# A second searched order for a fused convolution and mixer kernel, with three fewer pairs of blocks on ScalarE sums of squares

## The chip, the cores and the metric

The kernel runs on one core of one Trainium2 chip. The metric is the device time of one execution in microseconds (us); the kernel before takes 234.74 us (median of three, 234.25 to 235.0). The profiled execution took 234.25 us, and its trace spans 232.4 us from the first to the last instruction, so about 1.9 us of the time lie outside the span.

## What is computed

Two blocks follow each other on a sequence of S = 2048 rows of D = 512 numbers. The first is a long convolution with gates (A), the second a token mixer with an MLP (B), each behind a layer norm and with a residual sum. Cut to what matters:

```python
def A(q, k, v, shift_k, ssm_k, ssm_D):        # q is layernorm(x)
    k_shift = sum over 4 taps of the shifted k times shift_k
    kv = k_shift * v
    y = irfft(rfft(kv padded to 2S) * rfft(ssm_k padded to 2S))[:S]
    return q * (y + kv * ssm_D)

def B(x, w1, w2, w3, w4):
    h = gelu(layernorm(x) @ w1)
    g0..g3 = the four quarters of h's columns, moved by +1, -1, +2, -2 rows
    x1 = x + concat(g0..g3) @ w2
    return x1 + gelu(layernorm(x1) @ w3) @ w4          # w3: 512 x 1792, w4: 1792 x 512

h = x + A(layernorm(x), ...)
out = h + B(layernorm(h), ...)
```

## The kernel before

The Fourier transforms are done as matrix products in two steps each. The kernel builds a list of some 760 small tasks (a group of matmuls, one eviction, one load, one store), each with a closure that emits its instructions and with the engines that may run it. A long string, `ORDER`, then names every task by its number and the engine that gets it: P is TensorE, V VectorE, A ScalarE, G GpSimd, D the DMA queue of SyncE. A search on a host has made this string. Every engine executes its own tasks strictly in the order of the string, so a task whose input isn't there holds up all later tasks of the same engine, the DMA queue included.

```python
    def emit(self):
        made = set()
        for x in ORDER.split():
            n, e = int(x[:-1]), {o[0]: o for o in self.t[int(x[:-1])]["opts"]}[x[-1]]
            assert self.t[n]["deps"] <= made
            self.t[n]["fn"](e)
            made.add(n)
```

The names used below for the tasks of the convolution, for block groups `bl` or frequencies `kh`:

- h, k, v, q: loads. kf: a quarter of k that is loaded transposed by the DMA. F, K, FE, KE: first transform step of the filter and of kv and its eviction from PSUM; S, X: shifted k on TensorE and its product with v on VectorE; N, NE: transposes of k; FX, KX: exchanges over DMA between the two steps.
- G, GE, W, A, P, V, VE, VX: second step, product of the spectra (P, two VectorE operations), inverse step on TensorE (V), its eviction (VE) and the exchange back (VX). qs: row statistics of q.

Every PSUM tile of this part comes from one ring of four (`big`), so a task of TensorE also waits until the tile four allocations earlier is evicted. For an eviction the order chooses the engine:

```python
    def copy(e, o, i):
        if e == "A":
            nc.scalar.copy(o, i)
        else:
            nc.vector.tensor_copy(o, i)
```

In the mixer and MLP part, blocks of 128 rows pass through: J/I (last inverse step), Y (scale, ScalarE), H (residual, VectorE), statistics, hb (normalised h), LT/TE (its transpose), W (w1, TensorE), U (gelu), X (w2), S (x1), lb (normalised x1), L/E (its transpose), M (w3), G (gelu), O (w4), R, Z (sums on VectorE) and ZS (store of the output block). The variance of h and of x1 is taken in one of two ways, chosen per pair of blocks p by `HA` and `XA`:

```python
    HP, LP = 2, 1
    HA, XA = 4, (1, 2)
    # ... cut ...
    def summed(name, b, src, early, **kw):
        i = slice(b % 2, b % 2 + 1)
        if early:
            kw["accum_out"] = pair(name + "s", b // 2, 2, bufs=8)[:, i]
        nc.vector.scalar_tensor_tensor(out=src, **kw)
        if not early:
            stats(name, b, src)          # bn_stats and bn_aggr, both on VectorE

    def squares(name, b, src):           # task Q or SQ, only for early pairs
        def f(e):
            # ... cut ...
            nc.scalar.activation(jk[:], src, ACT.Square, bias=pair(name + "s", b // 2, 2, bufs=8)[:, i], scale=-float(D),
                                 accum_out=pair(name + "q", b // 2, 2, bufs=8)[:, i])
        return f
```

The transposes of the first `HP` = 2 pairs of h (blocks 0 to 3) and of the first pair of x1 are done on TensorE; all later ones go out to a scratch in HBM and come back through the transposing DMA:

```python
                if p < HP:
                    task(("LT", c), {"PE": 0.24}, transposes(("hb", c)), [("hb", c)], take="pt")
                    task(("TE", c), {"A": 0.48, "V": 0.33}, tcopy(("hb", c), hnT, c), drop=("LT", c))
                else:
                    task(("LT", c), {"D": 0.5}, stored(("hb", c), NB + c), [("hb", c)], lat=LAND)
            if p >= HP:
                task(("TE", b), {"D": 1.35}, flipped(hnT, NB + b - 1, 2, (b - 1) * P), [("LT", b - 1), ("LT", b)], lat=LAND)
```

The sum of an output block and its store are two tasks:

```python
            task(("Z", g, i), {"V": 0.7}, summed_up(g, i), [("R", bs[i])], drop=("O", g, i))
            task(("ZS", g, i), {"D": 0.4}, store(g, i), [("Z", g, i)], lat=2.0)
```

The product with w3 and its gelu have 56 tasks each (8 pairs of blocks by 7), the product with w4 has 17. PSUM gives the mixer part a ring of six tiles for matmuls and one of two for transposes.

Of the kernel before, what the change touches and what calls it, by code (L numbers as in the profile page):

```python
# [31 lines left out]
KB = 1024  # L32

ORDER = """
2D 4D 1D 39P 3D 41P 40A 12G 45P 42V 59P 5D 46A 14G 43P 60V 57P 44A 11G 7D 36P 58V 30P 13G 37A 52P 31V 48P 15G 53A 50P 6D
49A 61P 51V 54P 62A 69D 32P 55V 63P 33A 74P 64V 0D 76P 75V 8D 65P 77V 67P 66A 70P 16V 20G 68A 9D 82P 71V 17A 10D 34P 83V
27P 35A 98P 18V 21P 28A 72P 275V 19G 47D 99A 277V 22A 280V 102P 84P 302A 73V 103A 276V 92P 85V 86P 93A 78P 38D 281V 87A
283V 122P 23P 79V 123A 25P 56D 24A 26V 124P 100P 125A 282V 88P 80P 101A 284V 29D 285G 274V 89A 278V 90P 279G 81V 126P
91A 128P 129V 127A 112P 95D 114P 113A 96D 104P 115V 132D 140P 105A 110P 97D 141V 134P 111A 130D 116P 135V 106D 148P 117A
150P 94D 149V 136P 151A 107D 154P 137V 118D 142P 155A 138P 133D 143V 139V 152P 109D 164P 121D 153A 146P 165V 162P 108D  # L40
147A 190P 131D 163V 174P 191A 119D 158P 120D 175A 178P 159V 184P 179A 156P 192V 160P 185A 168P 180V 157A 193P 161A 169V
208P 194A 181P 186V 209A 196P 195D 182V 170P 197A 187P 210V 171A 183D 202P 176P 188A 198V 172P 203A 189D 211P 177V 173A
199P 204V 212A 214P 226P 215A 200V 213D 205P 227A 216V 201D 220P 206A 228V 221A 217P 207D 232P 222V 218A 229P 233A 244P
219D 230V 144P 245A 223P 234V 145A 231D 238P 166P 224A 246V 235P 239A 225D 250P 167V 236A 247P 240V 251A 262P 237D 248A
241P 252V 263A 256P 249D 242V 253P 257A 264V 268P 243D 254A 269A 258V 255D 265P 270V 266A 259P 293V 267D 260A 271P 288V
298P 261D 272A 289V 286V 273D 299P 303D 292V 300P 301P 287V 358P 304D 294V 307G 290V 359P 295V 306D 291G 360A 296V 365A
361V 297G 383A 308P 366V 388A 364A 384V 309P 369A 367P 389V 368P 334A 305D 362P 370V 387A 391P 335V 371G 339A 310A 337P
373G 340V 315A 372V 392A 376V 342P 316V 406P 343A 393V 377D 338A 374V 394G 311V 407P 375D 319A 317P 344V 396G 318P 408A
395V 397V 312P 431A 345G 409V 341P 398D 314A 378D 347G 412A 399A 320V 346V 446P 351V 321G 432V 348A 400D 429A 352P 323G
447P 353A 410P 322V 413V 467A 327G 349P 379P 450A 401D 324G 350A 328P 416V 381P 380A 430V 417G 448A 325P 329A 354P 419G  # L50
326A 433V 418V 420V 465A 356P 451V 434G 421D 422A 330P 355A 436G 423D 357A 435V 332P 439V 437G 382A 466V 440D 402P 331A
333A 438D 404P 403A 449V 424D 485P 405A 482P 452V 486V 453G 441D 497P 483V 487A 500P 455G 498V 484A 425P 501V 499A 427P
488V 426A 468V 489G 444P 502A 428A 442P 490V 445A 503V 491V 511P 504G 494A 469V 454V 458V 470G 456V 443A 492P 459D 505V
495P 512V 513P 493A 457D 472G 496A 523P 508A 514V 593P 509D 525P 460D 594A 524V 587P 595P 588A 526V 583P 596A 591P 527V
584A 597V 528G 463P 506V 592A 471V 475V 461P 473A 529V 598V 476D 532G 464A 585P 515V 474D 530V 462A 516G 531D 589P 586A
533D 517V 535P 518G 520A 537P 590A 477D 536V 599P 507D 538V 534D 519D 539V 521D 480P 540G 600V 602P 541V 544V 481A 601D
542V 545D 510D 543D 659P 522D 603V 655P 660A 604D 661P 656A 546D 611P 662A 664V 609P 663V 612A 637P 610A 627P 638A 683P
628A 671P 684A 685V 675P 672A 615P 686V 676A 679P 616A 631P 680A 649P 632A 607P 650A 617P 608A 639P 618A 620V 657P 619V
640A 642V 653P 658A 641V 478P 654A 629P 479A 605P 630A 547P 606A 571P 548V 559P 549P 572V 633P 613P 560V 634A 573P 614A
550V 673P 624P 674A 551V 574V 552G 575V 553V 554V 576G 635P 625V 556G 651P 577V 580V 636A 626D 578A 581D 561P 557D 652A  # L60
643P 579D 562V 563V 555D 564G 582D 665P 565V 568V 566G 644V 569D 645D 567D 668P 666V 667D 570D 749P 669V 745P 750A 751V
670D 737P 752V 746A 739P 738A 747P 740A 741P 748A 743P 742A 677P 744A 621P 678A 558D 756P 622V 623D 699P 757V 705P 758D
700A 703P 706A 707V 697P 708V 704A 695P 698A 701P 696A 646P 702A 717P 647V 721P 718A 648D 727P 722A 725P 728A 730V 719P
729V 726A 715P 720A 723P 716A 693P 724A 681P 694A 734P 682A 709P 735V 736D 731P 710V 711D 712P 732V 733D 690P 713V 714D
687P 691V 692D 753P 688V 689D 759P 754V 755D 760V 761D
"""

class Plan:
# [23 lines left out]
def kernel(  # L92
# [462 lines left out]
    xh1, x1 = hbm, q_sb  # L555

    HP, LP = 2, 1
    HA, XA = 4, (1, 2)
    pools = {}
    scr = ctx.enter_context(tc.tile_pool(name="scr", bufs=1, space=DRAM)).tile([2 * NB, P, D], BF16, name="scr")  # L560

# [348 lines left out]
```

## Time and profile before

| | us |
|---|---|
| time, median of three | 234.74 |
| span of the trace | 232.4 |
| TensorE busy | 217.2 |
| VectorE busy | 149.1 |
| ScalarE busy | 136.4 |
| GpSimd busy | 43.5 |

The page divides the span into 40 slices. TensorE's row alone looks full throughout, but a matmul that fills a stage paced by somebody else counts as busy as well, so the rows of the other engines have to be read beside it. The granted TensorE clock is full in every slice. All bulk transfers are issued by SyncE on one queue; they moved 34.9 MB. Three stages can be told apart: up to about 83 us the convolution, from there to about 102 us the start of the mixer, and after that the mixer and the MLP, which end at 229.4 us on TensorE.

### The profile page before, as it was taken

The page shows a single profiled execution, that of the slowest core. Times are in us where ns is not written, and L with a number is a line of the kernel's source. Part 1 is how long each engine was busy: PE and PEld are TensorE (multiplying, and loading weights), DVE is VectorE, ACT ScalarE, POOL GpSimd, SP SyncE. Part 2 cuts the span into 40 slices and gives each one's busy share as a digit, 9 for nine tenths or more (in the row PEclk, how much of TensorE's full clock was granted, in tenths as well). Part 3 has the DMA queues.
Part 4 walks back from the last instruction along what each step waited for, and adds up shares of the span by engine and source line. Part 5 has one row for each costly group of instructions (what it writes and reads, how often), then busy time and mean ns, then how long its engine had stood idle before and what let it go on. Part 6 is the DMA issues. An engine that isn't in the chain of part 4 may idle for free. (4 is left out here: it accounts for less than half of the span.)

```text
span 232.4 us, 4643 instructions
## 1 busy us (share of the span) xinstructions
PE 217.2 (93%) x1820; PEld 129.4 (56%) x1835; DVE 149.1 (64%) x331; ACT 136.4 (59%) x199; POOL 43.5 (19%) x80
## 2 busy tenths in 40 slices
PE   7999799999999988969999998999999999999994
PEld 2465344443332334557668567886645867874442
DVE  6775898999999987899898656007953130302221
ACT  3848869999999739968867235762220615440000
POOL 4931303000000132782435200000320000000000
PEclk9999999999999999999999999999999999999999
DMA  6999995971343599654333767000054300001111
GB/s 168 383 260 312 419 420 234 399 305 65 131 171 140 181 309 369 251 109 132 57 92 70 203 154 75 0 3 0 1 164 132 68 23 14 23 3 45 45 35 44
DMA packets 31079, 34.90 MB, mean 150 GB/s; under 512 B 17745, under 2 KB 26066, under 8 KB 29522
## 3 DMA queue, kind: packets, MB, share of 16 engines
q1 hardware_dynamic: 30912, 34.61, 47.7%
q8 instruction: 14, 0.23, 0.4%
q14 instruction: 7, 0.06, 0.1%
q10 hardware_dynamic: 146, 0.01, 0.0%
HBM read 12.59 MB, written 5.51 MB: 78 GB/s over the span
## 5 line engine op out<-in xcount | busy, mean ns | idle before, releaser
L778 ACT ACTIVATE ra<-mm 128x512 bf16<-128x512 f32 x56 | 33.4, 597 | 45.0 <-PE mm L772 45.0
L772 PE MATMUL mm<-rc,rb 128*128 128x256 bf16 x448 | 50.9, 273 | 1.0 <-DMA rc<-scr 1.0
L787 PE MATMUL mm<-rt,ra 128*128 128x512 bf16 (+1 forms) x232 | 49.2, 366 | 0.3
L772 PEld LDWEIGHTS <-rb 128*128 128x128 bf16 x448 | 43.8, 98 | 8.0 <-DMA rc<-scr 1.3
L794 DVE TENSOR_TENSOR ob<-mm,rd 128x512 bf16<-128x512 f32 (+1 forms) x17 | 11.2, 660 | 46.0 <-PE mm L787 46.0
L787 PEld LDWEIGHTS <-ra 128*128 128x128 bf16 x238 | 23.3, 98 | 24.5
L612 DVE SCALAR_TENSOR_TENSOR q_sb<-rd,cr,mm 128x512 bf16<-128x512 bf16 x16 | 11.7, 734 | 18.9 <-PE mm L733 18.7
L507 PE MATMUL pv<-rb,rt 64*128 64x512 bf16 x128 | 17.2, 378 | 1.1 <-ACT rb L269 0.5
L708 PE MATMUL mm<-rc,rf 128*128 128x256 bf16 x128 | 15.1, 273 | 1.9 <-DMA rc<-scr 1.9
L269 ACT CAST rb<-pw 128x1024 bf16<-128x1024 f32 x16 | 16.7, 1093 | 0.0
L269 ACT CAST ra<-pc 128x1024 bf16<-128x1024 f32 x14 | 13.6, 1021 | 2.8 <-PE pc L331 2.7
L733 PE MATMUL mm<-rf,rb 128*128 128x512 bf16 x60 | 14.9, 379 | 0.3
L386 PE MATMUL pk<-diag,rb 128*128 128x256 bf16 (+3 forms) x108 | 14.9, 285 | 0.3
L708 PEld LDWEIGHTS <-rf 128*128 128x128 bf16 x128 | 12.4, 98 | 3.9 <-issue 2.0
L714 ACT ACTIVATE rb<-mm 128x512 bf16<-128x512 f32 x16 | 9.2, 605 | 8.0 <-PE mm L708 6.9
L269 ACT CAST rb<-pv 128x1024 bf16<-128x1024 f32 x12 | 13.1, 1094 | 0.3 <-PE pv L507 0.2
L612 DVE SCALAR_TENSOR_TENSOR rd<-q_sb,qmv,z 128x512 bf16<-128x512 bf16 x16 | 12.1, 772 | 1.7 <-ACT z L599 1.7
L599 ACT ACTIVATE z<-mm,qrs 128x512 f32<-128x512 f32 x16 | 10.4, 706 | 4.6 <-PE mm L588 4.6
L386 PEld LDWEIGHTS <-rb 128*128 128x128 bf16 x112 | 9.4, 98 | 6.2 <-issue 1.7
L395 DVE TENSOR_TENSOR xk<-pk,rb 128x1024 bf16<-128x1024 f32 x8 | 9.7, 1212 | 4.9 <-DMA rb<-in_A_v_dram 2.6
L269 ACT CAST rc<-ph 128x1024 bf16<-128x1024 f32 x11 | 10.9, 1019 | 2.7 <-PE ph L331 2.6
L507 PEld LDWEIGHTS <-rt 64*128 64x128 bf16 x128 | 5.9, 94 | 11.4 <-issue 5.0
(170 smaller groups left out, 303.7 us busy)
## 6 DMA issues: line engine op xcount, KB each, us to landing
rd<-rc SPq DMA_DIRECT2D x16, 256.0 KB, 4.9
rc<-ra SPq DMA_DIRECT2D x16, 256.0 KB, 2.5
ra<-rb SPq DMA_DIRECT2D x16, 256.0 KB, 2.4
ra<-in_A_ssm_k_dram SPq DMA_DIRECT2D x4, 512.0 KB, 5.9
rb<-in_A_v_dram SPq DMA_DIRECT2D x2, 1024.0 KB, 8.6
q_sb<-in_A_q_dram SPq DMA_DIRECT2D x2, 1024.0 KB, 10.7
out_dram<-ob SPq DMA_DIRECT2D x15, 128.0 KB, 1.8
rt<-in_B_w_dram SPq DMA_DIRECT2D x1, 1792.0 KB, 9.5
```

The costliest lines, as they stand in the source:

```text
L269: nc.scalar.copy(o, i)
L386: nc.tensor.matmul(pk[:, i, P * (m + lo):P * (m + hi + 1)], lhsT=kT[:, c, b, KX0:] if b >= 0 else kT[:, c, NB + b, KX0 - 1:KX0 - 1 + P], r ...
L395: nc.vector.tensor_tensor(out=tl["xk", bl][:, :, cs].rearrange("p b (c x) -> p b c x", c=2), in0=tl["pk", bl, ch][:].rearrange("p c (b x) ...
L507: nc.tensor.matmul(ps[:, t, :], lhsT=tt[hs, min(x, 2), kh, :], rhs=pr[hs, x // 2, x % 2, :], start=(x == 0), stop=(x == 3))
L599: nc.scalar.activation(z[:], tl["y", b][:], ACT.Identity, bias=1.0, scale=qrs[:, b:b + 1])
L612: nc.vector.scalar_tensor_tensor(out=src, **kw)
L708: nc.tensor.matmul(pw_[:, j * 256:(j + 1) * 256], lhsT=w1_sb[:, k, m * P:(m + 1) * P], rhs=hnT[:, k, p * 256:(p + 1) * 256], start=(k == 0 ...
L733: nc.tensor.matmul(px[:], lhsT=shifted(m, b), rhs=w2_sb[:, m, :], start=(m == 0), stop=(m == DC - 1))
L772: nc.tensor.matmul(pg[:, j * 256:(j + 1) * 256], lhsT=w3_sb[:, k, fc * P:(fc + 1) * P], rhs=lnT[:, k, g * 256:(g + 1) * 256], start=(k == ...
L778: nc.scalar.activation(gbuf[:, g % 4, 2 * f:2 * f + 2, :], tl["g", g, f][:].rearrange("p (j x) -> p j x", j=2), ACT.Gelu_apprx_tanh)
L787: nc.tensor.matmul(po[:, 0:n], lhsT=gbuf[:, g % 4, fc, i * P:(i + 1) * P], rhs=w4_sb[:, fc, lo:lo + n], start=(fc == 0), stop=(fc == FC - 1))
L794: nc.vector.tensor_tensor(out=ob[:, 0:n], in0=tl["o", 2 * g + i, lo][:, 0:n], in1=xh1[:, order[2 * g + i], lo:lo + n], op=ADD)
```

## The change

The string is replaced by the result of another search, in which the output stores are steps of their own that are issued when their sum is ready. The kernel before has the same tasks for the sums and stores (Z and ZS above); what differs in the diff is the string and the two constants that choose how the variances are taken. `HA` goes from 4 to 3 pairs of h and `XA` from the pairs 1 and 2 of x1 to the pair 1 alone. Nothing else changes. The same values are computed, with four sums of squares fewer on ScalarE and four statistics more on VectorE.

The diff, with all but the first line of each string cut:

```diff
 ORDER = """
-2D 4D 1D 39P 3D 41P 40A 12G 45P 42V 59P 5D 46A 14G 43P 60V 57P 44A 11G 7D 36P 58V 30P 13G 37A 52P 31V 48P 15G 53A 50P 6D
-... (33 more lines)
+3D 2D 1D 48P 4D 54P 49A 14G 52P 55V 41P 5D 53A 13G 45P 42V 43P 46A 12G 7D 34P 44A 11G 36P 35V 59P 37A 15G 30P 60V 57P 6D
+... (33 more lines)
 """
@@ -555,7 +555,7 @@
     HP, LP = 2, 1
-    HA, XA = 4, (1, 2)
+    HA, XA = 3, (1,)
     pools = {}
```

Decoded, the parts of the two strings that the prediction speaks of (task names as above, the engine in front):

```
SyncE, loads       before: h2 k0 h1 h3 k1 v0 k2 kf3 h0 v1 q0 q1 FX2 FX1 FX3 FX0
                   after:  h3 h2 h1 k0 k1 v0 k2 h0 kf3 v1 q0 FX1 FX3 FX2 q1 FX0
SyncE, weights     before: w1 w2 w4 w3, LT5 LT4 LT6 TE5 ...        (four weight loads, then stores of h)
                   after:  w2 w4 w3, LT5 LT4, w1, TE5 LT6 ...
VectorE, early     before: X1.0 X1.1 an X0.0 X3.0 sg ...   after: X1.0 NE2.0 an X1.1 X2.0 sg X0.0 ...
TensorE, mixer     before: J3 LT3 I3 LT2 W2.0 LT1 W2.1 LT0 W1.0 W1.1 ...
                   after:  LT3 J3 LT2 I3 W1.0 LT0 W2.0 LT1 W1.1 W2.1 ...
TensorE, first M   before: M0 (x5) W6 W6 M0 M0 X10 X11 O0.0 W7.1 O0.1 M3 M3 M3 M1 M1 M2 ...
                   after:  M0 (x5) W6 W6 M0 M0 X10 M1 O0.1 X11 M1 O0.0 M3 M3 M1 M1 M2 ...
SyncE, x1          before: L5 TE13 .. L8 L9 TE15 L4 E9 L6 L7 ZS0.0 L11 E5 L10 E7 ZS0.1 E11 ...
                   after:  TE13 L4 L5 E5 L9 L8 E9 L6 L7 ZS0.1 E7 L10 LT15 ZS0.0 L11 LT14 E11 TE15 ...

moves between engines (number of tasks on ScalarE / VectorE / GpSimd):
                        before         after
GE (evict, 16)          9 / 7          10 / 6
VE (evict, 16)         12 / 4          13 / 3
fe (evict, 1)           1 / 0           0 / 1
KE (evict, 16)         14 / 2          13 / 3
FE (evict, 16)         11 / 5          12 / 4
NE (evict, 6)           3 / 3           1 / 5
Q, SQ (squares)        12 / -           8 / -
hb (scale h, 16)        4 / 9 / 3       3 / 6 / 7
lb (scale x1, 16)       4 / 8 / 4       6 / 3 / 7
cr (small, 8)           - / 0 / 8       - / 3 / 5
fill-in matmuls on TensorE: 11 groups of four before, 12 after
```

More of the change, by code (lines that the diff above doesn't have):

```diff
@@ L34 @@
 ORDER = """
-2D 4D 1D 39P 3D 41P 40A 12G 45P 42V 59P 5D 46A 14G 43P 60V 57P 44A 11G 7D 36P 58V 30P 13G 37A 52P 31V 48P 15G 53A 50P 6D
[L36 to L64, printed above, removed]
@@ L65 @@
-687P 691V 692D 753P 688V 689D 759P 754V 755D 760V 761D
+3D 2D 1D 48P 4D 54P 49A 14G 52P 55V 41P 5D 53A 13G 45P 42V 43P 46A 12G 7D 34P 44A 11G 36P 35V 59P 37A 15G 30P 60V 57P 6D
+31A 32P 58V 61P 33A 50P 0D 62V 39P 51V 63P 40A 74P 69D 64V 67P 75V 65P 8D 76P 66V 68A 20G 16V 78P 9D 77V 21P 17A 70P 79V
+38D 22A 18V 27P 104P 71V 302A 82P 56D 276V 28A 274V 98P 105A 72P 83V 99A 47D 277V 23P 73V 25P 19G 24A 84P 281V 26A 10D
+280V 86P 85V 88P 87A 100P 101V 89A 29D 126P 102P 127A 282V 92P 80P 103A 283V 93A 275V 109D 90P 278V 107D 81V 128P 279G
@@ new lines @@
+91A 122P 129V 112P 123A 96D 114P 113A 97D 124P 115V 94D 134P 125A 110P 95D 135V 140P 111A 106D 116P 141V 130D 138P 117A
+148P 139V 136P 149A 118D 154P 137V 119D 142P 155A 174P 121D 143V 150P 175A 133D 146P 151V 162P 108D 147A 178P 131D 163V
+179A 190P 184P 191A 284V 180V 164P 158P 185A 120D 156P 159V 165A 132D 181P 192V 157A 196P 152P 182A 186V 193P 197A 183D
+208P 153V 194A 187P 198V 209A 202P 195D 166P 203A 188V 199P 167A 210V 189D 214P 200A 160P 285G 168P 204V 215A 211P 169A
+161V 226P 212A 216V 205P 227A 213D 220P 206A 217P 228V 221A 232P 201D 170P 218V 207D 233A 229P 222V 171A 244P 176P 219D
@@ new lines @@
+230A 234V 172P 245A 223P 177V 173A 231D 235P 246V 224A 238P 250P 239A 236V 247P 251A 240V 237D 262P 248A 144P 252V 241P
+263A 225D 256P 145V 242A 249D 253P 257A 264V 243D 268P 269A 258V 265P 254A 270V 259P 266A 255D 289V 260A 271P 267D 286V
+298P 261D 272A 293V 287V 273D 299P 304D 294V 300P 301P 295V 358P 288V 306D 290V 359P 292V 291G 365A 296V 297G 360A 366V
+387A 308P 307G 361V 383A 369A 388V 309P 364A 362P 305D 339A 370V 368P 315A 384V 371G 390P 389P 334A 340V 310A 385P 372V
+335V 343A 404P 376G 311V 338A 374G 405P 377D 316V 312P 429A 373G 313P 375D 344V 391V 319A 367P 430V 345G 317P 314A 341P
@@ new lines @@
+336P 392G 410A 303D 363P 346V 351V 406A 348V 394G 352P 427A 320V 393V 444P 395V 378D 353A 321G 411V 397A 349P 396D 445P
+350A 398D 322V 407V 446A 324G 354P 448A 327G 325P 355A 414V 379P 428V 326A 415G 399D 463A 328P 356P 329A 431V 416V 465A
+381P 418V 464V 432G 420A 419D 332P 382A 421D 434G 330P 380A 433V 437V 333A 435V 402P 438D 449V 331A 436D 357A 400P 347G
+403A 422D 480P 447V 417G 401A 483P 439D 481V 497P 484V 495P 482A 450V 423P 498V 485A 451G 425P 424A 440P 486V 452V 426A
+453V 487G 496V 454A 442P 456G 441A 509P 455D 443A 488V 489V 492G 499V 507P 457D 510V 500G 490P 493P 519P 491A 494A 508V
@@ new lines @@
+521P 458D 587P 501V 520V 502A 504G 591P 588A 583P 503D 592A 522V 505D 581P 584A 585P 523V 466V 524G 459P 582A 506D 586A
+461P 525V 460A 594V 528G 579P 511V 462A 323V 526G 589P 529D 580A 531P 590A 527D 605P 532V 598P 606A 593V 530D 512G 513V
+514A 533P 516A 599V 515D 607P 467V 534V 517D 468G 600D 595P 608A 535V 469V 470V 536G 518D 473G 537V 538V 655P 540G 596V
+539D 474D 657P 471G 656A 597D 601P 541D 658A 660V 472D 603P 659V 602A 633P 604A 542D 625P 634A 629P 626A 475D 609P 630A
+627P 610A 651P 628A 677P 652A 667P 678A 679P 668A 673P 680A 681V 476P 682V 674A 478P 477A 671P 479A 675P 672A 545P 676A
@@ new lines @@
+569P 546V 543P 631P 570V 669P 632A 647P 544V 670A 611P 547V 557P 648A 567P 613P 612A 568V 649P 614A 645P 571V 650A 558V
+572G 620P 646A 548G 615V 573V 576V 574G 549V 577D 550A 635P 552G 575D 551D 617P 636A 638V 553D 637V 616V 578D 621V 555P
+618V 622D 554D 623P 556V 653P 624A 619D 686P 559V 654A 560G 561V 564A 565D 639P 687V 688D 693P 640V 691P 694A 641D 689P
+692A 642P 690A 664P 643V 644D 701P 665V 699P 702A 703V 666D 695P 704V 700A 661P 696A 562A 563D 739P 662V 743P 740A 663D
+566D 735P 744A 745P 736A 741P 746A 748V 737P 747V 742A 733P 738A 717P 734A 723P 718A 755P 724A 726V 725V 715P 756V 721P
@@ L66 @@
+757D 716A 719P 722A 697P 720A 713P 698A 711P 714A 708P 712A 730P 709V 710D 727P 731V 732D 683P 728V 729D 705P 684V 685D
+749P 706V 707D 752P 750V 751D 753V 754D
 """
```

## The prediction

> **What bounds the kernel now.** I read the page's forty slices first, for the stages.
>
> ```profile
> PE   7999799999999988969999998999999999999994
> ...
> DVE  6775898999999987899898656007953130302221
> ACT  3848869999999739968867235762220615440000
> ...
> DMA  6999995971343599654333767000054300001111
> ```
>
> TensorE (PE) looks full throughout, but in slices 7 to 14 VectorE and ScalarE are full as well, and in the first six and from slice 14 to 16 the DMA row is. A table of busy time by stage settles which of them paces what.
>
> ```profile
> 0.00:40.00 40.00, 35.64 (x396) 18.73 (x401) 30.58 (x66) 28.18 (x31) 15.59 (x37) 1.00 0.94 314
> 40.00:80.00 40.00, 38.35 (x352) 15.32 (x349) 39.51 (x62) 39.15 (x43) 0.66 (x2) 1.00 0.52 201
> 80.00:100.00 20.00, 17.23 (x193) 8.93 (x192) 17.36 (x59) 15.40 (x34) 8.63 (x15) 1.00 0.84 285
> ```
>
> The columns are TensorE matmul, weight load, VectorE, ScalarE, GpSimd, clock, DMA share and GB/s. From 0 to 40 us the DMA is 94% busy: loads. From 40 to 80 us VectorE (39.51 us) and ScalarE (39.15 us) have no gap: evictions and spectral products. From 80 to 100 us nothing is full but the DMA (weights); 5.7 us of TensorE's 17.2 are fill-in matmuls. From 101.77 us to 229.4 us TensorE is busy 125.95 of 127.63 us. So the end is set by when TensorE enters that last stretch, the work in it, and the waits in it. The list of TensorE's waits has the rest:
>
> ```profile
> PE mm L708 <- DMA rc<-scr: 1.9, 1, 1.9
> PE ph L331 <- DVE xk L395: 1.4, 1, 1.4
> ...
> PE mm L772 <- DMA rc<-scr: 1.0, 1, 1.0
> ```
>
> Three waits of note: one for a DMA-transposed h just before 101.77 us, one early in the convolution (at 25.02 us), one for a transposed x1 at 142.34 us. The chain of work that ended last names the last of these: a piece of 5.53 us `DMA rc<-scr` from 136.77 us, then TensorE nearly alone to 229.35 us and one sum of 0.42 us.
>
> **What the Trainium skill says.** (1) "Perfetto Trace Analysis", section Identifying the Most-Contended Engine: matmul busy time does not show nearness to the roofline, occupancy of VectorE and ScalarE does; the section on strategy adds that regimes have different limits. The trace agrees: 38.35 us of matmul busy in the stage whose two full engines are others. (2) "DMA: Bandwidth & Descriptors", Queues, rings and completion order: descriptors are consumed in ring order on each DMA engine. In the trace the first store of h, 128 KB, is issued at 91.92 us behind the weight loads and lands after a median of 3.9 us in that stage, against 1.8 us over the whole run; agrees. (3) "SBUF — State Buffer", Who interferes with whom: a VectorE operation with a two-port mode or two SBUF inputs and a GpSimd operation lock each other out for a whole instruction. At 126.48 us a VectorE scaling of lb took 729 ns beside a GpSimd one of 1201 ns, against 411 ns otherwise; agrees.
>
> **The change, stage by stage.** The stores of outputs cost nothing either way: between 189.76 and 230.16 us SyncE has nothing else to issue. So I weigh the string and the two constants.
>
> *Convolution, 0 to 83 us.* Loads: v1 is the tenth load in both strings, so it should land near 23.7 us as before (issued 16.77, landing 6.9 later). VectorE's new order puts X2.0, which needs v1, ahead of X0.0: VectorE idles longer there than the 2.6 us it did. TensorE then reaches K1.3 and waits for that ring tile until about 24.9 us, with four shift groups S and fourteen F done; before, it resumed at 25.02 us with four S, thirteen F and one K. Even. FX0 comes some 4 us earlier, since F0.1 and F0.2 go first, but the K evictions on ScalarE still end at about 44.6 us (my count of nine of them at 1.02 us from 35.4) against 44.2. From there to the last eviction (80.3 us) the two engines bind. ScalarE: one GE and one VE more, one fe less, +1 eviction at a spacing of 0.90 us (starts 59.50, 60.40 in a dense run): +0.9. VectorE: -1 GE, -1 VE, +1 fe at 1.14 us spacing: -1.1. ScalarE feeds the last products, VectorE ends them, so about half of the 0.9 reaches the end: **+0.5 us**, uncertain by 1.5.
>
> *Start of the mixer, 83 to 102 us.* Here is the gain. Before, w1, w2, w4 and w3 (4.6 MB) drain until about 97.5 us, the stores of blocks 4 and 5 queue behind them, TE5 is issued at 98.41 us, and W2.0, TensorE's first w1 task, needs it: the wait of 1.9 us. Three things move.
> - W1.0, whose h is transposed on TensorE, is now first. Its chain: H at 93.8 to 95.2, offset from GpSimd, hb3 and hb2 at 95.4 to 96.2, transposes, copies on ScalarE behind Q1, Q0, Y9, Y8, Y10 (93.7 to 97.5), TE3, hb7, TE2: about 99.5 us.
> - One weight of 0.5 MB goes behind stores LT5 and LT4. At 4.6 MB in 16.7 us (81.0 to 97.7) that is 1.9 us, so these land near 96.5 instead of 98.4; then w1 itself ends near 98 and TE5 lands near 100 to 100.5 instead of 101.77. hb5 and hb4 go to GpSimd (952 ns each, against 411 ns on VectorE), but one after the other right after the offset at 91.25, so LT4 still leaves at about 93.5 against 93.1.
> - With Q6 and Q7 off ScalarE (0.73 + 0.21 us each), Y0 to Y3 come earlier; VectorE pays two bn_stats and two bn_aggr (0.69 + 0.18 us).
>
> So W1.0 starts near 99.5 to 100 us, LT0, W2.0 and LT1 follow without waiting, and by 101.77 us some 2 us of w1 work are done that were all still ahead before: **-2.0 us**.
>
> *Dense stretch.* Its matmuls are the same 127 us. The 0.98 us wait should go: M2 needed E7, held on the DMA queue behind L10; now E7 stands behind ZS0.1. Counted from the end of X10 as zero: sum of S10 to 1.65, xm3 2.55, lb7 done 4.15, its store lands at about 6.3, E7 lands at 9.8 to 11.8 (3.5 median, 5.5 the long one); M2 is reached at 0.87 + 3.05 + 1.75 + 3.05 + 3.5 = 12.2. Clear, with little to spare. But M1 now comes right at zero and needs E5: S7 and S6 with their statistics (1.5 us each) stand ahead of xm2 on VectorE, so lb4 and lb5 are ready at -7.6, stored at -5.4, E5 lands at -1.9 to 0.1. And E15, issued after store ZS3.0, lands 4.6 to 6.6 us after O3.0, while seven M7 of 0.87 us give 6.1. I allow 1.0 us for these new waits: **-1.0 + 1.0 = 0**. VectorE in 100 to 142 us (35.13 of 42 us busy) gets four statistics of 0.87 and loses eight scalings of 0.41: about even. GpSimd gets seven scalings more (about 0.95 us), and with them lockouts.
>
> Sum: 234.74 + 0.5 - 2.0 + 0 = 233.2 us.
>
> **Rivals.** (a) *The head of the DMA queue*: any late task on SyncE's strict order delays all behind it, and LT15, LT14 and w1 now stand elsewhere. W1.0 needs w1, whose issue waits for LT4: were hb4 late by 3 us, w1 would land after 101 us and the whole gain would be gone. For it: SyncE's waits in before are long (up to 6.6 us for a store of h). Against: chain times above leave 1 us. It makes 235 to 237. (b) *GpSimd becomes the bound of the start*: seven hb of 0.95 us plus four powers of 1.1 us lie on the way to W. For it: GpSimd was busy 10.23 of 18.97 us from 82.8 to 101.77, and lockouts stretch a scaling to 1.2. Against: only hb4, hb5, hb0, hb1 are needed before W1.1. It would eat the 2 us: about 235. (c) *TensorE hides everything*: starts are earlier, yet X and U wait in turn for VectorE and ScalarE, and the gain shrinks to 0: 234.7. (d) *The convolution runs better than counted*, since FX0 and the first KX are earlier and q1 is out of the way of FX: 231.5.
>
> **Range and chances.** All steps are reorderings of a schedule that already has only some 11 us of TensorE waits in sum; a gain of 4.7 us (2%) would need half of these back, and a loss of as much would need a new stall longer than any now there. The errors of the three stages, about 1.5, 1.5 and 1.0 us, give about 2.3 us together, so 230.2 to 236.2 for 8 in 10. Faster by over 2%: 0.09; slower by over 2%: 0.06; between: 0.85.
>
> **What would show it.** Right: the `PE mm L708 <- DMA rc<-scr` wait of 1.9 us is gone or under 0.5, and the first L708 matmul comes before 100.5 us; evictions of the convolution end between 80 and 82 us; from the first L708 matmul to the end of TensorE it is 126 to 128 us; VectorE waits 4 us or more for v before 24 us. Wrong: L708 begins after 102 us with a wait for a weight load or for GpSimd, or L772 waits several us for DMA. What would upset the number most is a stall in the convolution that my count of order positions doesn't see, since four ring tiles couple all engines there.

## The result, and the profile after

The changed kernel takes 232.13 us (median of four runs, 231.62 to 232.45) against 234.51 us for the kernel before on the same chip: a ratio of 0.9894 (95% interval 0.9868 to 0.9921). That is 1.1% faster and within 2%. The trace's span went from 232.4 to 230.5 us.

The picture by stages is that of before: loads first, then VectorE (DVE) and ScalarE (ACT) nearly full, then the DMA full again with the weights, then TensorE (PE) alone. The stage table of the kernel after gives the sizes (stretch, length, busy time of TensorE matmul, weight load, VectorE, ScalarE and GpSimd with instructions, clock, DMA share, GB/s):

```profile
0.00:40.00 40.00, 37.24 (x416) 19.56 (x424) 32.82 (x68) 28.10 (x31) 14.57 (x36) 1.00 0.97 327
40.00:80.00 40.00, 37.06 (x333) 14.69 (x331) 37.27 (x61) 38.45 (x42) 1.01 (x1) 1.00 0.48 185
80.00:100.00 20.00, 17.30 (x197) 9.17 (x196) 18.47 (x58) 13.66 (x29) 12.02 (x15) 1.00 0.94 292
```

VectorE is busy 37.27 us in the second stage, where it was 39.51: it now has a gap there. In the third, GpSimd went from 8.63 to 12.02 us, mostly through the two scalings moved to it (2.88 us). Both could matter; the experiments e9 and e7 gain nothing that can be told from noise there. TensorE's waits in the kernel after (line, what it waits for: us in all, times, longest):

```profile
PE pw L419 <- DMA rc<-ra: 1.3, 1, 1.3
...
PE ptx L686 <- DVE rd L674: 1.0, 1, 1.0
PE mm L588 <- ACT z L599: 0.9, 2, 0.7
...
PE mm L708 <- ACT rb L714: 0.2, 1, 0.2
```

All three waits shown of the kernel before have gone: `rc<-scr` at L708 (1.9 us) and at L772 (1.0 us), and the 1.4 us at L331 for `xk`. The longest is new, 1.3 us for an exchange of the convolution (`rc<-ra`). Not all of this is the order's doing: in e3 below, which has the same convolution, the 1.4 us at L331 are there and the wait for the exchange isn't. The wait of 1.0 us at L686, for a scaled h on VectorE, lies in the start of the mixer; in the kernel before it is 0.4 us. The timeline of TensorE (start, duration, engine, line, operation) shows the point where the old wait was, in the kernel before:

```profile
101.77 1.03 PE L708 MATMUL mm<-rc,rf 128*128 128x256 bf16 x8 [1.91 <-DMA rc<-scr]
```

and in the kernel after:

```profile
99.16 0.61 PE L588 MATMUL mm<-ra,f_71 32*128 32x512 bf16 x8
99.90 1.03 PE L708 MATMUL mm<-rc,rf 128*128 128x256 bf16 x8
101.17 0.40 PE L686 MATMUL ptx<-ident,rd 128*128 128x128 bf16 x4 [0.23 <-POOL rd L674]
101.40 1.04 PE L708 MATMUL mm<-rc,rf 128*128 128x256 bf16 x8
```

The first w1 task runs at 99.90 us, straight behind the last inverse matmuls, and by 101.77 a good part of the second is done as well. From here on I split each span at two marks: the first inverse matmul of the mixer (first L588) and the first w1 matmul (first L708); the last end is that of TensorE. All in us:

| kernel | first L588 | first L708 | end of TensorE | L588 to L708 | L708 to end |
|---|---|---|---|---|---|
| before | 82.83 | 101.77 | 229.33 | 18.94 | 127.56 |
| after | 82.91 | 99.90 | 227.40 | 16.99 | 127.50 |

In these two executions the convolution ends within 0.1 us of each other, the dense stretch is as long as before, and 1.95 us are gone between the marks.

### The profile page after: what moved, and what is told of

Same layout as the page of the kernel before. It is cut to its first block, busy times and chain, and to the rows that moved or that the text cites. A ratio compares the mean times of both kernels' runs of the same rounds, so it can differ in the third digit from the quotient of the medians.

```text
span 230.5 us, 4640 instructions
## 1 busy us (share of the span) xinstructions
PE 217.8 (95%) x1823; PEld 129.6 (56%) x1839; DVE 151.5 (66%) x334; ACT 134.7 (58%) x191; POOL 50.3 (22%) x81
## 3 DMA queue, kind: packets, MB, share of 16 engines
q1 hardware_dynamic: 30912, 34.61, 47.5%
## 4 chain that ended last, share of the span: by engine, by line
PE 62%; DVE 15%; DMA 8%; SPq 5%; ACT 5%; issue 2%; POOL 2%; ACTq 0%; DVEq 0%
PE mm L772 21%; PE mm L787 21%; PE mm L733 5%; PE pv L507 4%; SPq L367 4%; PE mm L708 4%; DMA q_sb<-in_A_q_dram 4%; DVE qst L465 2%; DMA ssk_bf<-in_A_shift_k_dram 2%; DMA rc<-ra 2%; PE pw L419 2%; DVE xk L395 2%; PE wm L530 2%; DVE rd L271 2%; DVE rd L612 1%
## 5 line engine op out<-in xcount | busy, mean ns | idle before, releaser
L772 PE MATMUL mm<-rc,rb 128*128 128x256 bf16 x448 | 51.2, 273 | 0.1
L772 PEld LDWEIGHTS <-rb 128*128 128x128 bf16 x448 | 43.8, 98 | 7.4
L794 DVE TENSOR_TENSOR ob<-mm,rd 128x512 bf16<-128x512 f32 (+1 forms) x17 | 11.2, 660 | 44.6 <-PE mm L787 44.2
L269 ACT CAST rb<-pw 128x1024 bf16<-128x1024 f32 x16 | 16.4, 1066 | 1.2 <-PE pw L419 1.2
L474 POOL TENSOR_TENSOR qrs<-qrs,mhalf 128x4 f32<-128x4 f32 x4 | 4.1, 1018 | 56.1 <-DVE qrs L470 56.1
L708 PE MATMUL mm<-rc,rf 128*128 128x256 bf16 x128 | 15.1, 273 | 0.3 <-ACT rb L714 0.2
L269 ACT CAST ra<-pc 128x1024 bf16<-128x1024 f32 x13 | 12.5, 1018 | 2.4 <-PE pc L331 2.2
L708 PEld LDWEIGHTS <-rf 128*128 128x128 bf16 x128 | 12.4, 98 | 2.6 <-DMA rc<-scr 0.5
L269 ACT CAST rc<-ph 128x1024 bf16<-128x1024 f32 x12 | 11.7, 1016 | 3.4 <-PE ph L331 3.3
L269 ACT CAST rb<-pv 128x1024 bf16<-128x1024 f32 x13 | 13.6, 1079 | 0.0
L648 POOL TENSOR_TENSOR rr<-uw,mhalf 128x4 f32<-128x4 f32 x8 | 9.6, 1204 | 14.0 <-DVE hm L636 11.6
L419 PEld LDWEIGHTS <-rf 128*64 128x64 bf16 x128 | 6.3, 108 | 10.8 <-issue 5.7
```

What stands on the lines that cost most here:

```text
L419: nc.tensor.matmul(ps[64 * t:64 * t + 64, r, :], lhsT=ftab[:, kh, r, t, :], rhs=z[:, kh, t, :], start=True, stop=True)
L708: nc.tensor.matmul(pw_[:, j * 256:(j + 1) * 256], lhsT=w1_sb[:, k, m * P:(m + 1) * P], rhs=hnT[:, k, p * 256:(p + 1) * 256], start=(k == 0 ...
L772: nc.tensor.matmul(pg[:, j * 256:(j + 1) * 256], lhsT=w3_sb[:, k, fc * P:(fc + 1) * P], rhs=lnT[:, k, g * 256:(g + 1) * 256], start=(k == ...
L794: nc.vector.tensor_tensor(out=ob[:, 0:n], in0=tl["o", 2 * g + i, lo][:, 0:n], in1=xh1[:, order[2 * g + i], lo:lo + n], op=ADD)
```

## The experiments

Five things had to be told apart: whether the gain sits in the convolution's order or the mixer's; whether the order of the weight loads or that of the first w1 tasks makes it; whether the constants `HA` and `XA` carry any; whether GpSimd is on the path; and what binds next. The same convolution, instruction for instruction, put its first L588 at 82.91, 83.76, 83.45, 83.69, 83.00 and 83.16 us in six profiled executions (the kernel after, e1, e3, e4, e5, e7), so single profiles are compared from that mark on, and times by their intervals.

**One half of the string at a time.** The tasks of the convolution and of the rest have separate numbers, so each half of one string goes with the other half of the other.

```diff
 e1: tasks of the convolution as after, the rest as before; HA, XA = 4, (1, 2)
 e2: tasks of the convolution as before, the rest as after; HA, XA = 3, (1,)
```

> The convolution's tasks (up to its last fill-in matmuls) in the new order, the mixer's tasks in the old order with the old constants. Theory A (the gain is made at the start of the mixer; the convolution ends at the same time in both): no gain, 234.2 to 235.0 us, first inverse matmul of the mixer (L588) near 82.9 us, first w1 matmul (L708) near 101.8. Rival B (the new convolution order brings it): 232.0 to 233.0 us.

> The convolution's tasks in the old order, the mixer's in the new order with the new constants. Theory A: the whole gain, 231.8 to 232.6 us, L708 first at 99.8 to 100.1. Rival B: 234 us or more.

The new convolution alone: 234.89 us, ratio 1.0025 (0.9998 to 1.0051). The new mixer alone: 231.82 us, ratio 0.9903 (0.9864 to 0.9941). The timeline of e1 has the wait,

```profile
102.59 1.03 PE L708 MATMUL mm<-rc,rf 128*128 128x256 bf16 x8 [1.81 <-DMA rc<-scr]
```

and that of e2 doesn't:

```profile
99.81 1.03 PE L708 MATMUL mm<-rc,rf 128*128 128x256 bf16 x8
```

From L588 to L708 it is 18.83 us in e1 (before 18.94) and 16.99 in e2 (after 16.99). The whole gain is in the mixer's half, its order with its constants. The convolution's order gives none, for all that it shuffles; by the first L588 it rather costs half a microsecond, since four executions with the old order of the convolution (before, e2, e6, e11) have that mark at 82.52 to 82.89 us, earlier than all six with the new one.

**Which of the moves: weights, or first w1 tasks.** In the kernel after, three things were changed back singly and together. The order of SyncE's loads, and that of TensorE's first w1 tasks (W1.0 has its h transposed on TensorE, W2.0 over the DMA):

```diff
 e3:  SyncE    - w2 w4 w3 LT5 LT4 w1 TE5
               + w2 w4 w3 w1 LT5 LT4 TE5
 e4:  TensorE  - W1.0 LT0 W2.0
               + W2.0 LT0 W1.0        (and U2.0 ahead of U1.0 on ScalarE)
 e5:  both
```

> The changed kernel with one move undone: the load of w1 goes back ahead of the stores of blocks 5 and 4, so that all four weight loads stand before them. Theory A with the weight order as its cause: the stores land later and the transposing DMA is issued near 98 us instead of 96.5, the second w1 task (block pair 2) waits about 1 us, time 232.6 to 233.4. If w1's place in the queue carried the whole gain: 234. If it is worth nothing: 232.1 plus or minus 0.2.

> The changed kernel with TensorE's first w1 task for block pair 2 (transposed by the DMA) again ahead of that for pair 1 (transposed on TensorE), and their first gelus swapped with them. In the changed kernel the transposing DMA is issued at 96.47 us and took 3.4 us to land before, so it is there at about 99.9 us, when TensorE is ready for it: theory A with the weight order as its cause says 232.1 to 232.6. If the order of the first w1 tasks carried the gain: 233.5 to 234.

> The changed kernel with both moves of the mixer's start undone: w1 loaded ahead of the stores of blocks 5 and 4, and the first w1 task that of block pair 2. Theory A: the wait for the transposing DMA comes back, 1.5 to 2 us, so L708 first at about 101.5, time 233.6 to 234.2. If the start gains by the lighter ScalarE instead: 232.1 to 232.6.

| kernel | TE5 issued | first w1 tasks | L588 to L708 | wait at L708 | time, ratio (95%) |
|---|---|---|---|---|---|
| after | 96.47 | W1.0 | 16.99 | none | 232.13, 0.9894 (0.9868 to 0.9921) |
| e3 | 98.35 | W1.0 | 16.99 | none | 231.84, 0.9906 (0.9872 to 0.9940) |
| e4 | 97.40 | W2.0 | 17.76 | 0.90, ScalarE's `z` named | 231.84, 0.9913 (0.9879 to 0.9946) |
| e5 | 98.08 | W2.0 | 18.40 | 1.53, DMA `rc<-scr` | 233.12, 0.9944 (0.9921 to 0.9967) |

The issue of TE5 is read in the timeline of SyncE's queue; in the kernel after it stands there behind the two stores of h (L695) and w1 (L277):

```profile
93.31 1.67 SPq L695 DMA_DIRECT2D scr<-rd  x2
95.01 0.44 SPq L277 DMA_DIRECT2D rf<-in_B_w_dram  x1
96.47 1.29 SPq L699 DMA_TRANSPOSE rc<-scr  x1
```

and in e3, with w1 ahead of the stores:

```profile
93.84 1.66 SPq L695 DMA_DIRECT2D scr<-rd  x2
98.35 1.28 SPq L699 DMA_TRANSPOSE rc<-scr  x1
```

ScalarE's `z` in the row of e4 need not be the true cause: 97.40 us and the 3.7 us that such a transpose takes to land (median from 98 to 112 us in the kernel after) make 101.1, just ahead of its L708 at 101.45.

So the half megabyte behind the stores does bring the transpose forward: counted from the first mark, it is issued 13.56 us after L588 in the kernel after and 14.90 in e3. But with W1.0 first, nobody waits for it: e3 is as quick to L708 as the kernel after. Only with W2.0 first does the weight order count, 0.64 us (18.40 against 17.76). The task order counts 1.41 us with the weights early (e5 against e3) and 0.77 with w1 late (e4 against the kernel after). The two moves hide the same wait, so their gains don't add, and the one that removes the need beats the one that shortens it. The times resolve only part of this: e5 keeps about half of the gain (0.9944), while the intervals of e3, e4 and the kernel after overlap almost whole, so the 0.77 us of e4 rests on its profile alone.

The counterpart is the task order alone, put into the kernel before:

```diff
 e11 (from before):  TensorE  - W2.0 LT1 W2.1 LT0 W1.0
                              + W1.0 LT1 W2.1 LT0 W2.0        (and U1.0, U2.0 exchanged)
```

> The kernel before with one change: the first w1 task is that of block pair 1, placed as soon as its copies are done, and that of pair 2 comes after (their first gelus swapped). Nothing else moves, the constants and the weights stay. In before the last of those copies ends at 101.08 us, so pair 1 can start 0.7 us before the 101.77 us at which pair 2 could: 233.6 to 234.0 us, L708 first near 101.1. If the order of these tasks alone were enough for the whole gain: 232.3.

232.86 us, ratio 0.9953 (0.9927 to 0.9979). The timeline of e11:

```profile
100.81 1.03 PE L708 MATMUL mm<-rc,rf 128*128 128x256 bf16 x8 [1.26 <-ACT rc L269]
```

L588 to L708 is 18.29 us, 0.65 less than before: the wait for the DMA has become one for ScalarE's copy of the transposed h (`rc`, L269). ScalarE still has Q6 and Q7 and stands in the old order, so W1.0's own input is late. By the ratio of times, one exchange of two tasks gives a bit under half of the gain; how it does that is read below, at the clock. That the remainder needs ScalarE's and VectorE's order of the start to fit it is argued, since no run moved those tasks alone. From e5 to before (18.40 to 18.94) the last 0.54 us come from moves that I haven't separated.

**The constants alone.**

```diff
 e6 (from before):  - HA, XA = 4, (1, 2)
                    + HA, XA = 3, (1,)       order without Q6 Q7 SQ4 SQ5
```

> The kernel before with only the two constants changed: three pairs of h and the pair 1 of x1 with sums of squares, the four squares taken out of the old order, nothing moved. Theory A: no gain, 234.3 to 235.0, since the wait for the transposing DMA behind the weights stays. Rival C (relief of ScalarE by four squares of 0.9 us is what brings the gain): 232.5 to 233.5.

The ratio is 1.0008 (0.9971 to 1.0045), taken over the 7 of its 22 executions that lie within 1.5% of its fastest: no gain. The median of all 22 is 236.42 us, above the 234.95 of the kernel before in that round. Four passes less on ScalarE (two pairs of blocks, one of h and one of x1, where the title says three) are worth nothing in the old order. Whether the new order gains by them is not shown, since no run took the new order with the old constants.

**What the wait at L708 costs besides its length.** For every execution the record has the TensorE clock that was granted, as a mean over the span (1 is full speed). In the runs e1 to e12, and in the kernel before as it was run beside them, it is either 0.998 or more, or 0.993 or less, with nothing between. How often it is the lower one goes with the wait at L708:

| kernel | wait at L708 in its trace | executions with the lower clock |
|---|---|---|
| after, e2, e3, e7, e8, e9, e12 | 0.5 or less | 0 of 41 |
| e4 | 0.90 | 0 of 8 |
| e11 | 1.26 | 3 of 20 |
| e5 | 1.53 | 1 of 22 |
| e1 | 1.81 | 16 of 22 |
| before (all its executions beside e1 to e12) | 1.91 | 88 of 123 |
| e6 | 2.67 | 17 of 22 |
| e10, below | 3.87 | 17 of 20 |

One trace of the old order shows where the clock goes, that of e6 (mean clock 0.992). Here is the row of the clock in forty slices, and TensorE's timeline:

```profile
PEclk9999999999999999979999999999999999999999
102.52 1.86 PE L708 MATMUL mm<-rc,rf 128*128 128x256 bf16 x8 [2.67 <-DMA rc<-scr]
```

By stretches of 1 us its clock is 1.00 up to 102 us, then 0.57, 0.50, 0.50 and 0.72, and 1.00 again from 106 us. So it falls 2.3 us after TensorE's last matmul (which ended at 99.85) and stays at half for 3.4 us; over 235 us that makes a mean of 0.993. The traces of before, e1, e5 and e11 are of executions with the higher clock, so that the loss sits at the same place in their other executions is inferred and not shown. The exchange of e11 alone took the share from 28 of 39 (before, in its round) to 3 of 20.

The times read differently with this. Run beside e1 to e4, the kernel before takes 233.28 us at the higher clock (median of 11) and 234.79 at the lower (19), while e2, e3 and e4 take 231.82 to 231.84, always at the higher. At equal clock the new order of the mixer is then worth about 1.4 us, and about 1 us more in the medians is clock that is no longer lost. By these medians what e5 and e11 gain is mostly the clock: at the higher one e5 takes 233.11 us (21 executions) against 233.45 for before in its round (12), and e11 232.82 (17) against 232.79 (11). And e5 at 233.11 is 1.2 us behind e7, of the same round (231.90 us, the new order but for two scalings, see the next experiment): the two moves that e5 undoes carry most of the gain at equal clock. One reservation: if the length of the wait decides which executions of before keep the clock, those are the ones with short waits, and the medians at equal clock understate what the order itself saves.

**GpSimd's scalings back on VectorE.**

```diff
 e7 (from after):  - hb5, hb4 on GpSimd
                   + hb5, hb4 on VectorE
```

> The changed kernel with the scalings of blocks 5 and 4 on VectorE (0.41 us each) in place of GpSimd (2.88 us for the two). Their stores are issued 1 to 1.5 us earlier (before 93.8 us), the w1 load behind them too. If the GpSimd scalings are on the path that sets L708's start: 231.2 to 231.9. If the weights' bytes in the DMA queue or the copies on ScalarE set it: 232.1 plus or minus 0.3.

The stores leave 0.82 us earlier, counted from L588 (9.58 us after it instead of 10.40), L708 comes 16.64 us after L588 (16.99), and the time is 231.90 us, ratio 0.9881 (0.9838 to 0.9923), the same as the kernel after within the intervals. So GpSimd is not the bound, although the chain of work that ended last, in the kernel after, runs through its two scalings:

```profile
91.58 2.88 POOL rd L674 x2
```

A line in that chain is a suspect and no verdict: taken out, it gave at most 0.35 us. The wait at L686 fell with it, from 1.00 to 0.32 us.

**What binds next.** The end of the convolution stands against two things: fill-in matmuls, which only keep TensorE busy, and row statistics of q on VectorE. e8 drops the last two groups of four fill-ins, which compute nothing that is used:

```diff
 e8 (from after):
-        task(("wm", NH + i), {"PE": 0.5}, warm, ...
+        task(("wm", NH + i), {"PE": 0.5}, lambda e: None, ...
```

> The changed kernel without the last two groups of four fill-in matmuls between the convolution and the mixer (results unused; nothing of the computation is left out). In both traces the mixer's first inverse matmul starts right after them, at 82.83 and 82.91 us, though the convolution's evictions end at different times. If they set that start: L588 first at 81.8 to 82.3 and 231.3 to 231.8 us. If the exchange back over DMA sets it: 232.1 plus or minus 0.2.

231.40 us, ratio 0.9871 (0.9830 to 0.9913). Its TensorE timeline:

```profile
81.22 2.51 PE L588 MATMUL mm<-ra,f 32*128 32x512 bf16 x34
```

The first L588 is at 81.22 instead of 82.91 us: 1.69 us of fill-ins had stood in front of real work. But only 0.55 us arrive at H, the first residual sum on VectorE. In the kernel after it had to wait for its input `z`:

```profile
85.71 0.75 DVE L612 SCALAR_TENSOR_TENSOR rd<-q_sb,qmv,z 128x512 bf16<-128x512 bf16 x1 [0.71 <-ACT z L599]
```

and in e8 it follows directly upon the last statistics of q:

```profile
85.08 0.17 DVE L470 TENSOR_SCALAR qrs<-qmv 128x4 f32<-128x4 f32 x1
85.16 0.75 DVE L612 SCALAR_TENSOR_TENSOR rd<-q_sb,qmv,z 128x512 bf16<-128x512 bf16 x1
```

So VectorE takes over as the bound within half a microsecond. At the end of this trace nothing is left of the lead: TensorE ends at 227.40 us, as in the kernel after, with a wait of 0.46 us for `rc<-scr` at 105.86 us that the kernel after doesn't have. e9 moves two of the statistics into a hole of 1.4 us that VectorE has at 47.5 us:

```diff
 e9 (from e8):  VectorE  - qs.11, qs.8 late
                         + qs.11, qs.8 ahead of the first product P0
```

> The changed kernel without the last two groups of fill-in matmuls (as in the run with fewer fill-ins) and with two of the eight row statistics of q that VectorE does between the convolution and the mixer moved into its gap of 1.4 us at 47.5 us. With fewer fill-ins alone the first inverse matmul came 1.7 us earlier, but VectorE's row statistics ran until 85.08 us and H began 0.55 us earlier only. If those statistics are the next bound: H begins near 84.4 us, L708 near 98.7, time 230.6 to 231.4 us. If the transposing DMA behind the weights binds there: same as with fewer fill-ins, 231.2 to 231.8.

H now waits 0.68 us for `z` again, so the statistics don't bind any more. L588 to L708 is 17.33 us, where it was 17.92 in e8. The convolution of this execution ended later (L588 at 82.63), and the time is 231.60 us, ratio 0.9887 (0.9836 to 0.9938): no more than the kernel after.

The last suspect is the queue of weights, and e10 and e12 move w4 (1.8 MB, needed only in the MLP) behind the stores and transposes of h:

```diff
 e10 (from e9):  SyncE  - w2 w4 w3 LT5 LT4 w1 TE5
                        + w1 w2 w3 LT5 LT4 TE5 LT6 LT7 TE7 w4
 e12 (from e9):         + w1 w2 w3 LT5 LT4 TE5 ... TE9 TE11 w4
```

> As the run with the statistics in the hole, and w1, w2, w3 loaded first and w4 (1.8 MB, needed only by the product with w4 near 129 us) after the transposes of block pairs 2 and 3. The stores of blocks 5 and 4 then have 1.3 MB less ahead of them: the first transposing DMA is issued at or before 95.5 us and no w1 task waits for it. If the weights' bytes bind the start: another 0.5 us faster than the run with the statistics in the hole. If the copies on ScalarE for pair 1 bind: the same within 0.3 us, and if w4's late load disturbs the later transposes: slower, with a wait of a w1 or w3 task for rc<-scr.

> As the run with w4 late, but w4 is issued only after the transposes of block pairs 4 and 5 (near 109 us), when the next store of h comes at about 115 us. In the run with w4 late, L708 began at 98.66 us instead of 99.90, and all its loss came after: the stores of blocks 8 to 11 stood behind w4's 1.8 MB, the transposes of pairs 4 and 5 were issued at 110.5 us instead of 107.5 and TensorE waited 3.9 us. If that is the whole account: L708 first at 98.4 to 99.0, no wait of L708 for rc<-scr, 230.5 to 231.3 us. If the late w4 disturbs the transposes of x1 as well: a wait of L772 for rc<-scr and 232 us or more.

From L588 to L708 nothing changes: 17.34 us in e10 and 17.38 in e12, where e9 has 17.33, although TE5 is issued 13.73 and 13.76 us after L588 instead of 15.94. So the bytes of the weights don't bind this start. What does is not shown. A lead is the wait of 1.00 us at L686 for VectorE's scaled h, which these three traces have like the kernel after: e7, where it is 0.32 us, has the shortest stretch (16.64 us). Behind L708 the place of w4 matters. e10 reaches L708 at 98.66 us and is still slower than before: 236.99 us, ratio 1.0072 (1.0041 to 1.0104). Its SyncE timeline:

```profile
100.61 0.58 SPq L277 DMA_DIRECT2D rt<-in_B_w_dram  x1
103.27 2.99 SPq L695 DMA_DIRECT2D scr<-rd  x4
110.52 2.58 SPq L699 DMA_TRANSPOSE rc<-scr  x2
```

The four stores of h stand behind w4, and the profile's list of DMA issues for 98 to 116 us (KB each, median us to landing) gives their landing in e10:

```profile
scr<-rd SPq DMA_DIRECT2D x4, 128.0 KB, 6.1
```

against, in the kernel after, for 98 to 112 us:

```profile
scr<-rd SPq DMA_DIRECT2D x6, 128.0 KB, 2.1
```

The Trainium skill says so in "DMA: Bandwidth & Descriptors", Queues, rings and completion order: each DMA engine takes the descriptors in the order of its ring. The trace agrees, with 6.1 us against 2.1. The transposes of those blocks leave at 110.52 us (107.51 in the kernel after), and TensorE stands still for them:

```profile
114.21 2.10 PE L708 MATMUL mm<-rc,rf 128*128 128x256 bf16 x9 [3.87 <-DMA rc<-scr]
```

From L708 to the end e10 takes 133.60 us, 6.10 more than the kernel after: 3.87 of wait and 2.2 of something else. The stage table of e10 (the clock is the third figure from the right) shows what:

```profile
112.00:114.20 2.20, 0.00 (x0) 0.00 (x0) 2.06 (x10) 0.00 (x0) 1.48 (x3) 0.63 0.90 182
114.20:118.00 3.80, 3.79 (x18) 2.72 (x19) 0.92 (x3) 0.75 (x2) 1.55 (x2) 0.50 0.12 26
```

TensorE's clock was halved during the wait and came back at 119.4 us. The 5.2 us from 114.21 on at half clock are worth 2.6 us of work, an estimate that covers the 2.2. The Trainium skill's "TensorE: Matmul & The Clock Gate", section on the HAM clock gate, gives an idle window of about 3.4 us after which the clock is at half. The trace agrees on the half, 0.50, but not on the time: the last matmul ended at 110.34 us, and a mean of 0.63 from 112.00 to 114.20 puts the fall at about 112.6, after 2.2 us of idleness; in e6 it came after 2.3 us, in a wait of only 2.67.

In e12 w4 goes behind those transposes too, and of the wait at L708 0.41 us are left (at 122.46 us):

```profile
105.86 2.58 SPq L699 DMA_TRANSPOSE rc<-scr  x2
108.49 0.57 SPq L277 DMA_DIRECT2D rt<-in_B_w_dram  x1
```

Its TensorE timeline:

```profile
98.24 1.03 PE L708 MATMUL mm<-rc,rf 128*128 128x256 bf16 x8
```

TensorE ends at 225.95 us, 1.45 us before the kernel after, and the span is 229.0 us. All of that lead stands at the first mark already (L588 at 80.86 us, 2.05 us earlier than in the kernel after); the two stretches behind it are 0.39 and 0.21 us longer. The time is 231.88 us, ratio 0.9880 (0.9841 to 0.9920). In that one profile e12 is the best of all; by the intervals it is not told apart from the kernel after (0.9868 to 0.9921). Whether the last 1.5 us are real is left open.

## Why the prediction was right

The time predicted was 233.2 us; measured, 232.13. The sum was -1.5 us, and the measured difference is -2.4 in the time and -1.9 in the span. At equal clock, beside e1 to e4, it is about -1.4, close to the sum; the rest of the -2.4 is most likely the clock, which falls in most executions of the kernel before and for which the prediction had no step. The three terms as the traces give them, -1.95, -0.06 and +0.56 (a mean, see below), make -1.45 as well. So no term of the sum holds the 1.1 us by which the kernel came out below the predicted time. (The clock of each of the four executions behind the 234.51 us is not on record; the profiled one had the full clock and took 234.25 us, near the top of the 232.35 to 234.61 us that executions of before at the higher clock took later, so its trace may overstate the loss.) Step by step:

**Start of the mixer, -2.0 us: right in mechanism, and in size by the traces.** Measured 16.99 against 18.94 us, so -1.95. W1.0 came at 99.90 (predicted 99.5 to 100), TE5 was issued at 96.47 (the stores were to land at 96.5). Of its three parts, the prediction named the first w1 task and the weight behind the stores side by side; e3 shows that the first alone suffices; e4, with the weight's move alone, keeps all but 0.77 us of the stretch. The third, Q6 and Q7 off ScalarE, is worth nothing by itself (e6), but e11 shows ScalarE's copies as the next wait when the exchange is made in the old order.

**The dense stretch, 0: right.** 127.50 us from the first L708 to the end (predicted 126 to 128; before 127.56). The L772 wait for `rc<-scr` is gone, as computed. The new waits for E5 and E15, allowed 1.0 us, don't appear among TensorE's waits. That the stretch is only 0.06 us shorter all the same has two sides: idle time fell from 1.62 to 1.16 us, and the matmuls, 883 records instead of 884, were busy 126.34 us instead of 125.94. Why they took 0.4 us more is open. And e1, which keeps the old order of the mixer, has no L772 wait either, nor has e11, so that wait belongs partly to the execution.

**The convolution, +0.5: right in sum, wrong in its steps.** Measured +0.08 in the two executions compared; over the six and four executions named at e1 and e2 the mean of the mark went from 82.77 to 83.33 us, +0.56. So the half microsecond is there, though not by the steps that gave it. The prediction had v1 land "near 23.7 us as before (issued 16.77, landing 6.9 later)" and VectorE wait 4 us or more for it. The timeline of SyncE's queue after:

```profile
5.86 0.43 SPq L277 DMA_DIRECT2D ra<-in_A_ssm_k_dram  x1
6.33 10.06 SPq L367 DMA_TRANSPOSE rb<-in_A_k_dram  x4
16.44 0.58 SPq L277 DMA_DIRECT2D rb<-in_A_v_dram  x1
```

and before:

```profile
4.94 11.16 SPq L367 DMA_TRANSPOSE rb<-in_A_k_dram  x4
16.14 0.58 SPq L277 DMA_DIRECT2D ra<-in_A_ssm_k_dram  x1
16.77 0.44 SPq L277 DMA_DIRECT2D rb<-in_A_v_dram  x1
```

The same number of loads stand ahead of v1, but a filter load was moved from behind the transposed loads of k to before them. v1 is issued 0.33 us earlier and lands 5.2 us later rather than 6.9, at about 21.6 us; VectorE waits less for it, not more. Its list of waits, before and after:

```profile
DVE xk L395 <- DMA rb<-in_A_v_dram: 2.6, 1, 2.6
DVE xk L395 <- DMA rb<-in_A_v_dram: 1.4, 1, 1.4
```

So the step that failed is counting the place in the queue without what the places hold. A second step failed with it: the K evictions on ScalarE were to end at about 44.6 us, and the timeline of ScalarE after has

```profile
36.72 5.95 ACT L269 CAST ra<-pc 128x1024 bf16<-128x1024 f32 x6 [0.42 <-PE pc L331]
```

that is 42.67 us, 1.5 before the old 44.22. This lead was given back at the first wait shown of the kernel after:

```profile
47.26 1.49 PE L419 MATMUL pw<-rc,rf 128*64 128x512 bf16 x12 [1.32 <-DMA rc<-ra]
```

TensorE stands 1.32 us for an exchange there and is at 47.26 us where it was at 47.81 in the kernel before: of a lead of one microsecond (first L419 at 42.09 against 43.12), half is left. At the last eviction on ScalarE it is 80.14 us against 80.30, and the first L588 comes no earlier, behind the fill-ins. The eviction balance was off as well: VectorE's busy time from 40 to 80 us fell by 2.24 us (predicted 1.1), and ScalarE's fell by 0.70 where 0.9 more was expected. No run undid these evictions singly, so their share isn't shown; only the sum is, by e1.

**The rivals.** The head of the DMA queue (a) did not come: the two stores were issued from 93.31 to 94.98 us where LT4 was to leave at 93.5, since the scalings took 1.44 us each instead of 0.95, and the margin held. It did come in e10, by 3.87 us, when 1.8 MB instead of 0.5 stood in the way. GpSimd as the bound (b) is refuted by e7. Everything hidden (c) is refuted by the 1.95 us, of which TensorE's end shows 1.93. A better convolution (d), 231.5 us, named the right lead but not where it would be lost.

## What to carry to other kernels

When a late transfer holds up the first task of a long stretch, first look for another task that can go ahead and doesn't need it: here that exchange was worth 0.8 to 1.4 us between the marks, and bringing the transfer forward nothing once it was made. A saving in a stage reaches the end only if nothing waits there for another engine or for filler: follow it with a few marks on the engine that ends last, and compare from mark to mark, since two executions of the same instructions differed by up to 0.85 us at the first mark. Compare the granted clock of the executions as well before a difference of medians is given to the order alone: in before, with a wait of about 2 us, the executions with the lower clock took 1.5 us longer. And a load put ahead of small transfers in a strictly ordered queue is to be weighed by its bytes and by the wait behind it: 0.5 MB ahead of the stores of h was hidden, 1.8 MB cost 6.1 us.

## What the hardware did that was not expected

- A TensorE wait of 3.87 us cost 6.1 us, since the clock stood at 0.50 after it (e10). In the two traces with a lowered clock it fell 2.2 and 2.3 us after TensorE's last matmul and stayed at half for 6.8 and 3.4 us (e10, e6).
- Two GpSimd scalings of 128x512 in bf16 took 2.88 us beside VectorE, where the prediction had 0.95 each. Of the three sums on VectorE that overlap them, one took 1.09 us and the others 0.74 and 0.75.
- The issue of four transposed loads kept SyncE's queue for 10.06 and 11.16 us, and the plain loads behind them were issued only at 16.4 and 16.1 us (after and before).
- Without eight fill-in matmuls the first real matmul of the mixer began 1.69 us earlier (e8), and the clock stayed at 0.998 or more in all 6 executions.
